# Three reorderings in the opening stage of a fused sliding-window attention and leaky-ReLU kernel

## The chip, the cores and the metric

The kernel runs on one core of a Trainium2 chip. TensorE (PE in the profile; PEld for its weight loads) multiplies matrices, VectorE (DVE), ScalarE (ACT) and GpSimd (POOL) work on elements, and SyncE (SP) only issues transfers here. Transfers that must change type on the way (float32 in memory, bfloat16 on the chip) are issued by POOL and travel in one software queue; the plain ones are issued by SP and travel in one hardware queue. Both queues are served by the same 16 DMA engines. Each engine, SP included, runs its instructions in the order in which the program names them, and waits on semaphores for the others.

The metric is the device time of one execution in microseconds. The kernel before takes 308.22 us, the median of three runs from 307.94 to 308.43.

## The reference

Eight batches of eight heads, 576 tokens, 64 dimensions a head: attention in a band of 32 tokens to either side, and then a feed-forward layer with a leaky ReLU.

```python
scores = (1.0 / np.sqrt(D)) * np.matmul(q, k.transpose(0, 1, 3, 2))
mask = np.abs(pos[:, None] - pos[None, :]) <= 32
scores = np.where(mask, scores, -1000000000.0)
scores = scores - np.max(scores, axis=-1, keepdims=True)
attn = np.exp(scores)
attn = attn / (np.sum(attn, axis=-1, keepdims=True) + 1e-09)
x = np.matmul(attn, v).transpose(0, 2, 1, 3).reshape(B * S, H * D)   # 4608 x 512
h = x @ w_in                                                        # 512 x 2048
g = np.maximum(0.01 * h, h)
return (g @ w_out).astype(np.float32)                               # 2048 x 512
```

## The kernel before, in words

All of the order is written out by hand: the program is one long list of calls, and each call appends its instructions to the engines that it uses. Heads are taken in pairs (`NPAIR` is 4), so that two heads of 64 fill 128 partitions. Batch 0 and batch 1 are each cut into two halves of 288 tokens; a step of attention is one half of one pair, and steps 0 to 15 cover the two batches. Steps 0 to 3 are the first half of batch 0, 4 to 7 its second half, 8 to 11 the first half of batch 1. The other six batches go in blocks of 64 tokens and are not touched here.

One step `i` runs through these functions:

- `load_qk(b, p)` issues two transfers on SP, queries (`qf`) and keys (`kf`) of pair `p`, 288 KB each. With the argument `behind`, the named engine first writes one element of the target tile, so that SP's transfer waits until that engine has come to this place in its own order.
- `cast_qk` makes bfloat16 copies `qb` and `kb` (line 298); for batch 1 the queries on DVE, the keys on POOL.
- `transposes` turns both on PE (lines 340 and 344) and copies them out on ACT (line 352). `place_keys` spreads the keys of batch 1 into `kbd` on DVE (line 371).
- `score(i)` multiplies them (lines 440 and 447), ACT takes the exponential (line 452), POOL or DVE multiplies by the mask (line 454).
- `sums(i)` is `row_sums` on PE (line 479) and `inverse` on DVE, a reciprocal (line 509). For step 3 the sums are made in another way: `row_sums_by_quarters` (line 490), a short reciprocal (line 495), and `spread` (line 501, in float32), which brings the inverses back to full shape. `make_rows` prepares two constant tiles for that on POOL (lines 194 to 197).
- `product(i)` multiplies by the values (line 524) and `scaled(i)` multiplies by the inverse sums and writes `xT` (line 543).

The values arrive by `load_cast_v` (line 147, POOL's queue, one transfer a head), the weights by `load_w_in` (line 727, four chunks of 512 columns) and `load_w_out` (line 731, four chunks of 512 rows), also POOL's queue.

The feed-forward layer takes the tokens in groups; group `g` of the first four is one half of a batch. `h_mms` (line 567) makes one tile of h, 128 columns of w_in by 288 tokens, from four slices `c` of 128 dimensions; slice `c` needs the pair `c` of heads. `h_first(0)` makes the first four tiles of group 0 slice by slice, as a generator: each `next` emits one more part, so that the program can put other PE work between the slices. The four tiles take the four buffers of the pool `mmps`, which the transposes and the sums of steps 1 and 2 have used before. `o_pair` (line 653) makes the first two tiles of the output, in eight parts of four matmuls; part `(j, n)` needs chunk `n` of w_out. Before each part it calls `spend`, which inserts attention work of batch 1 by a count of turns.

The pools `"x"` and `"s"` in `xps` have one buffer each: a product waits until `scaled` has read the one before, and `row_sums` waits until the reciprocal before it has read its sums (for step 4, until `scaled(3)` has read what `spread` wrote).

Around line 837, after the first group, the program casts the loads of batch 1: DVE casts queries 0 and 1 there, and queries 2 and 3 in `second_pair(0)` and `second_pair(1)`. Behind the cast of queries 3 DVE has `place_keys` for pair 2, eight clearing writes of `set_ones` and `clear_k` (lines 261 to 267), and the reciprocal of step 8.

Of the kernel before, what the change touches and what calls it, by code (L numbers as in the profile page):

```python
# [16 lines left out]
def kernel(  # L17
# [15 lines left out]
    nc = tc.nc  # L33
# [7 lines left out]
    NPAIR = H // 2  # L41
# [26 lines left out]
    def load_qk(b, p, behind=None):  # L68

        for into, src, name in ((qf, q, "qf"), (kf, k, "kf")):
            t = fload.tile([128, 2 * RUN * D], FP32, name=f"{name}{p}")
            if behind is not None:
                behind.memset(t[0:1, 0:1], 0.0)
                behind = None
            heads = src[b, 2 * p:2 * p + 2]
            if b == 0:

                into[b, p] = t[:, 0:NB * D]  # L80
                nc.sync.dma_start(
                    out=into[b, p], in_=heads.rearrange("a (p c) d -> (a p) (c d)", c=NB))
                continue
            t = t[0:96].rearrange("p (a r) -> p a r", a=2)
            if b < BY_DMA:
                nc.sync.dma_start(out=t, in_=heads.rearrange("a (p c) d -> p a (c d)", c=RUN))
            elif into is qf:
                nc.sync.dma_start(
                    out=t.rearrange("p a (g e) -> p a g e", g=3),
                    in_=heads.rearrange("a (g p c) d -> p a g (c d)", g=3, c=2),  # L90
                )
            else:
                nc.sync.dma_start(
                    out=t.rearrange("p a (c d) -> p a c d", d=D),
                    in_=heads.rearrange("a (c p) d -> p a c d", p=96),
                )
            into[b, p] = t
# [45 lines left out]
    def load_cast_v(b, p, heads=range(2)):  # L143

        for a in heads:
            r = slice(64 * a, 64 * a + 64)
            nc.gpsimd.dma_start(  # L147
                out=vbd[b % 2][r, p, :, r],
                in_=v[b, 2 * p + a].rearrange("(c p) d -> p c d", p=64),
            )  # L150
# [42 lines left out]
    def make_rows():  # L193
        nc.gpsimd.memset(to_rows, 0.0)
        for a in range(2):
            nc.gpsimd.memset(to_rows[64 * a:64 * a + 64, 96 + 16 * a:112 + 16 * a], 1.0)
        nc.gpsimd.tensor_copy(
            out=from_rows.rearrange("p (u m) -> p u m", m=64),
            in_=ident_f[:, 0:128:16].unsqueeze(2).to_broadcast([128, 8, 64]),
        )  # L200
# [175 lines left out]
    def where(i):  # L376
        return i // 8, (i // 4) % 2, i % 4
# [6 lines left out]
    def score_blocks(i):  # L384
        p, bs = i % NPAIR, blocks_of(i)
        n = 2 * 64 * len(bs)
        lo = 512 * (i % 2)
        sc = ps[:, lo:lo + n].rearrange("p (a w c i) -> p a w c i", a=2, c=2, i=32)
        for w, (b, m) in enumerate(bs):
            tok = qz[b % 2][:, p, m // 3].rearrange("p a (c i) -> p a c i", c=2)  # L390
            at = 32 * (m % 3)
            nc.tensor.matmul(  # L392
                sc[:, :, w], kz[b % 2][:, p, 64 * m:64 * m + 128],
                tok[:, :, :, at:at + 32], start=True, stop=True,
            )
        e = attn.tile([128, 2 * HALF], BF16, name="e")
        nc.scalar.activation(out=e[:, 0:n], in_=ps[:, lo:lo + n], func=AF.Exp, scale=scale)  # L397
        pr = prob[:, i % NPROB].rearrange("p n i -> p (n i)")[:, 0:n]
        nc.gpsimd.tensor_mul(pr, e[:, 0:n], band.rearrange("p w c i -> p (w c i)")[:, 0:n])  # L399
        probs[i] = pr.rearrange("p (a w i) -> p a w i", a=2, i=64)  # L400
# [28 lines left out]
    def score(i, masked_by=nc.gpsimd):  # L429
        if i >= OLD:  # L430
            return score_blocks(i)
        b, hf, p = where(i)
        tok = qT[b][:, p, hf * HALF:hf * HALF + HALF]
        if b == 0:

            for a, n_, m in ((0, 0, 0), (1, 1, 0), (0, 0, 1), (1, 1, 1), (0, 0, 2),
                             (0, 1, 0), (1, 0, 0), (0, 1, 1), (1, 0, 1), (1, 0, 2)):
                blk, i0, n = WIN[hf][n_][m]
                r = slice(64 * a, 64 * a + 64)
                nc.tensor.matmul(  # L440
                    ps_v[r, n_, i0:i0 + n], first_keys[p][r, 64 * blk:64 * blk + 64],
                    tok[r, i0:i0 + n], start=True, stop=True,
                )
        else:
            for n_, blocks in enumerate(WIN[hf]):
                for blk, i0, n in blocks:
                    nc.tensor.matmul(  # L447
                        ps_v[:, n_, i0:i0 + n], kbd[b % 2][:, p, blk],
                        tok[:, i0:i0 + n], start=True, stop=True,
                    )  # L450
        e = attn.tile([128, 2 * HALF], BF16, name="e")
        nc.scalar.activation(out=e, in_=ps[:, P0:P0 + 2 * HALF], func=AF.Exp, scale=scale)  # L452
        pr = prob[:, i % NPROB]
        masked_by.tensor_mul(  # L454
            pr.rearrange("p n i -> p (n i)"), e, mask[hf].rearrange("p n i -> p (n i)"),
        )
        probs[i] = [pr, None, None]
# [27 lines left out]
    def row_sums_by_quarters(i):  # L485
        s = xps.tile([128, 512], FP32, name="s")
        pr = probs[i][0]
        for j in range(4):
            for n in range(2):
                nc.tensor.matmul(  # L490
                    s[:, 0:QUART], to_rows[:, 96 - 32 * j:224 - 32 * j],
                    pr[:, n, QUART * j:QUART * j + QUART],
                    start=(j == 0 and n == 0), stop=(j == 3 and n == 1),
                )
        nc.vector.reciprocal(quarters, s[:, 0:QUART])
        probs[i][2] = s

    def spread(i):
        s = probs[i][2]
        for j in range(4):  # L500
            nc.tensor.matmul(
                s[:, 128 + QUART * j:128 + QUART * j + QUART], from_rows[:, 128 * j:128 * j + 128],
                quarters, start=True, stop=True,
            )
        probs[i][2] = s[:, 128:128 + HALF]
# [11 lines left out]
    def product(i):  # L517

        b, hf, p = where(i)
        pr = probs[i][0]  # L520
        x = xps.tile([128, 512], FP32, name="x")[:, 0:HALF]
        parts = [(n_, *block) for n_ in range(2) for block in WIN[hf][n_]]
        for n_, blk, i0, n in parts:
            nc.tensor.matmul(  # L524
                x[:, i0:i0 + n], vbd[b % 2][:, p, blk, :], pr[:, n_, i0:i0 + n],
                start=(blk == parts[0][1]), stop=(blk == parts[-1][1]), skip_group_check=True,
            )
        if i in (1, 2, 3):

            to = kept[i] if i < 3 else recip.tile([128, HALF], FP32, name="r")  # L530
            nc.scalar.activation(out=to, in_=x, func=AF.Copy)
            x = to
        probs[i][1] = x
# [7 lines left out]
    def scaled(i):  # L541
        _, x, r = probs.pop(i)
        nc.vector.tensor_mul(place(i), x, r)
# [20 lines left out]
    def h_mms(g, f, h, cs):  # L564
        t0, n = GROUPS[g]
        for c in cs:
            nc.tensor.matmul(  # L567
                h[:, 0:n], w_in_bf[:, c, ts(f, 128)], xT[:, c, t0:t0 + n],
                start=(c == 0), stop=(c == DMC - 1),
            )  # L570
# [42 lines left out]
    def h_first(g):  # L613

        hs = [mmps.tile([128, 512], FP32, name="mm", tag="mm") for _ in range(4)]
        yield hs[0]
        for c in range(DMC):
            for f in range(4):
                h_mms(g, f, hs[f], (c,))
            if c == DMC - 1:  # L620
                for f in range(4):
                    h_out(g, f, hs[f])
            yield
# [102 lines left out]
    def load_w_in(f0, f1):  # L726
        nc.gpsimd.dma_start(out=w_in_bf[:, :, f0:f1], in_=w_in_r[:, :, f0:f1])  # L727
# [37 lines left out]
    cast_qk(0, 3, nc.scalar, nc.gpsimd)  # L765
    load_cast_v(0, 3, (1,))
    load_w_in(512, 1024)
    load_w_in(1024, 1536)
    sums(1)
    score(2, masked_by=nc.vector)  # L770
    next(first)
# [2 lines left out]
    product(0)  # L774
    scaled(0)
    make_rows()
    score(3)
    sums(2)
    product(1)
    score(4)  # L780
    product(2)
    row_sums_by_quarters(3)
    scaled(1)
    scaled(2)
    load_w_in(1536, 2048)
    clear_on_act(kbd[1][:, 1])
    h0 = h_first(0)
    h = next(h0)
    next(h0)
    product(3)  # L790
    score(5)
    spread(3)
    scaled(3)
    next(h0)
    next(h0)
    for p in range(NPAIR):
        load_qk(1, p, nc.gpsimd if p == 0 else None)
    load_w_out(0)
    nc.gpsimd.memset(kbd[1][:, 2], 0.0)
# [39 lines left out]
    clear_vf(2)  # L839
    cast_qk(1, 1, nc.vector)  # L840
    load_cast_v(1, 0)
    load_cast_v(1, 1, (0,))
    next(band_parts)
    for p in (2, 3):
# [123 lines left out]
```

## Time and profile before

| What | Before |
|---|---|
| median of three runs | 308.22 us |
| profiled execution, its own time | 308.76 us |
| span in its trace | 307.1 us |
| PE busy | 298.0 us (97%) |
| DVE busy | 221.7 us (72%) |
| ACT busy | 204.1 us (66%) |
| POOL busy | 201.5 us (66%) |
| granted TensorE clock | 1.00 |

The profile is one execution taken by the hardware profiler. Its times count from the start of the span; a row of a timeline gives the start, the duration, the engine, the line, the operation, the tiles, the count, and in brackets the idle time of that engine just before, with what ended it. Rows that begin with an `x8` or the like are several instructions merged. The duration of a merged PE row runs to the modelled end of its last matmul, so the next row starts before it ends; what PE spends is read from start to start. A transfer appears as its issue; "DMA to landing" is the time from that issue to the arrival of the last byte.

### The profile page before, as it was taken

What the parts mean: (1) busy time and instruction counts of PE and PEld (TensorE: products, weight loads), DVE (VectorE), ACT (ScalarE), POOL (GpSimd) and SP (SyncE); (2) the same over time, 40 slices, a digit from 0 to 9 for tenths busy, and PEclk for the clock granted to TensorE, in tenths of its full rate; (3) what the DMA queues carried; (4) which work ended last, traced back from release to release, by engine and by line L of the source; (5) the groups of instructions that cost most, each with busy time, mean ns of one, the idle gap of its engine ahead of it and who ended that gap; (6) DMA issues with size and microseconds to landing.
All of it is one profiled execution on the core that took longest, in us unless ns stands there. A gap on an engine that the chain in (4) does not pass through costs nothing.

```text
span 307.1 us, 6942 instructions
## 1 busy us (share of the span) xinstructions
PE 298.0 (97%) x2616; PEld 193.5 (63%) x2646; DVE 221.7 (72%) x302; ACT 204.1 (66%) x423; POOL 201.5 (66%) x258
## 2 busy tenths in 40 slices
PE   8799999999999999999999999999999999999996
PEld 3577855676757777676768685858555555444643
DVE  6879579597888987897799777898689766743000
ACT  7876964564946677685858585849589548843731
POOL 8989799867999996889577366579757533110000
PEclk9999999999999999999999999999999999999999
DMA  7999999998999999999969984994950110001002
GB/s 248 205 183 268 264 152 218 218 209 145 208 186 215 191 256 188 190 192 228 208 151 237 226 177 113 204 204 106 196 121 1 36 68 36 0 34 72 34 31 74
DMA packets 121506, 48.31 MB, mean 157 GB/s; under 512 B 96256, under 2 KB 115968, under 8 KB 121472
## 3 DMA queue, kind: packets, MB, share of 16 engines
q1 hardware_dynamic: 107776, 42.48, 67.9%
q0 software_dynamic: 13696, 5.38, 14.5%
q8 instruction: 21, 0.34, 0.5%
q14 instruction: 13, 0.11, 0.1%
HBM read 36.70 MB, written 9.44 MB: 150 GB/s over the span
## 4 chain that ended last, share of the span: by engine, by line
PE 86%; DMA 6%; POOL 5%; issue 1%; ACT 1%; POOLq 0%; ACTq 0%
PE mm L637 38%; PE mm L567 36%; DMA w_out_bf<-in_moe_w_out_dram 6%; PE ps L392 4%; PE s L410 2%; POOL set L147 2%; PE x L410 2%; PE mm L653 2%; POOL w_in_bf L727 1%; PE x L524 1%; POOL prob L454 1%; PE ps L447 0%; POOL kb L298 0%; ACT gT L575 0%; PE s L479 0%
## 5 line engine op out<-in xcount | busy, mean ns | idle before, releaser
L567 PE MATMUL mm<-xT,w_in_bf 128*128 128x256 bf16 (+3 forms) x956 | 133.5, 294 | 0.2
L637 PE MATMUL mm<-w_out_bf,gT 128*128 128x512 bf16 (+2 forms) x537 | 122.5, 373 | 1.3
L419 DVE RECIPROCAL r<-r 128x256 f32<-128x256 f32 (+1 forms) x56 | 95.0, 1696 | 34.3 <-ACT r L418 33.7
L567 PEld LDWEIGHTS <-w_in_bf 128*128 128x128 bf16 x960 | 91.4, 98 | 29.6
L399 POOL TENSOR_TENSOR prob<-e,band 128x512 bf16<-128x512 bf16 (+1 forms) x56 | 62.6, 1118 | 56.8 <-ACT e L397 55.6
L637 PEld LDWEIGHTS <-gT 128*128 128x128 bf16 x560 | 52.1, 98 | 54.1
L575 ACT ACTIVATE gT<-mm 128x288 bf16<-128x288 f32 (+2 forms) x112 | 49.9, 479 | 12.4 <-PE mm L567 9.9
L397 ACT ACTIVATE e<-ps 128x512 bf16<-128x512 f32 (+1 forms) x56 | 32.4, 579 | 27.6 <-PE ps L392 24.6
L642 ACT ACTIVATE o_sb<-mm 128x512 f32<-128x512 f32 (+2 forms) x35 | 20.5, 585 | 39.2 <-PE mm L637 38.9
L598 ACT ACTIVATE gT<-mm 128x512 bf16<-128x512 f32 x64 | 35.7, 596 | 5.3 <-PE mm L567 3.9
L509 DVE RECIPROCAL r<-s 128x288 f32<-128x288 f32 x13 | 25.4, 1957 | 3.8 <-PE s L476 2.4
L423 DVE TENSOR_TENSOR xT<-x,r 64x256 bf16<-64x256 f32 (+1 forms) x56 | 24.4, 436 | 3.7 <-PE mm L567 0.5
L298 POOL CAST kb<-kf 96x768 bf16<-96x768 f32 (+1 forms) x30 | 25.0, 832 | 3.0 <-DMA kf<-in_k_dram 2.5
L423 DVE TENSOR_TENSOR xT<-s,r 64x256 bf16<-64x256 f32 (+1 forms) x56 | 24.4, 435 | 3.3
L324 DVE COPY set<-kT 64x576 bf16<-64x576 bf16 x48 | 21.4, 446 | 1.7 <-DMA kT<-qb 0.8
L392 PEld LDWEIGHTS <-set 128*128 128x128 bf16 x216 | 16.8, 98 | 9.2
L392 PE MATMUL ps<-set 128*128 128x128 bf16 x216 | 21.2, 219 | 0.0
L303 POOL CAST set<-vbuf 128x640 bf16<-128x640 f32 x24 | 17.2, 717 | 4.5 <-DMA vbuf<-in_v_dram 2.8
L298 POOL CAST qb<-qf 96x768 bf16<-96x768 f32 x24 | 19.7, 820 | 0.1
L454 POOL TENSOR_TENSOR prob<-e,mask 128x576 bf16<-128x576 bf16 x13 | 16.5, 1275 | 2.9 <-ACT e L452 2.8
L410 PEld LDWEIGHTS <-set 128*128 128x128 bf16 x432 | 18.0, 98 | 0.5
L304 POOL CAST set<-vbuf 64x512 bf16<-64x512 f32 x24 | 14.6, 610 | 1.5
(104 smaller groups left out, 242.2 us busy)
## 6 DMA issues: line engine op xcount, KB each, us to landing
qf<-in_q_dram SPq DMA_DIRECT2D x32, 288.0 KB, 5.5
kf<-in_k_dram SPq DMA_DIRECT2D x32, 288.0 KB, 6.1
out_dram<-o_sb SPq DMA_DIRECT2D x35, 256.0 KB, 2.9
vbuf<-in_v_dram SPq DMA_DIRECT2D x15, 256.0 KB, 4.6
w_in_bf<-in_moe_w_in_dram POOLq DMA_DIRECT2D x4, 512.0 KB, 8.4
w_out_bf<-in_moe_w_out_dram POOLq DMA_DIRECT2D x4, 512.0 KB, 15.6
vbuf<-in_v_dram SPq DMA_DIRECT2D x10, 192.0 KB, 4.4
set<-in_v_dram POOLq DMA_DIRECT2D x16, 72.0 KB, 6.4
```

The costliest lines, as they stand in the source:

```text
L298: eng.tensor_copy(out=to, in_=tok)
L392: nc.tensor.matmul(sc[:, :, w], kz[b % 2][:, p, 64 * m:64 * m + 128], tok[:, :, :, at:at + 32], start=True, stop=True,)
L397: nc.scalar.activation(out=e[:, 0:n], in_=ps[:, lo:lo + n], func=AF.Exp, scale=scale)
L399: nc.gpsimd.tensor_mul(pr, e[:, 0:n], band.rearrange("p w c i -> p (w c i)")[:, 0:n])
L410: nc.tensor.matmul(x[:, a, w], vw[b % 2][:, p, m, a:a + 2].rearrange("p n d -> p (n d)"), pr[:, a, w], start=True, stop=True,)
L419: nc.vector.reciprocal(r[:, 0:n], r[:, 0:n])
L423: nc.vector.tensor_mul(xT[rows, p, t0:t0 + n].rearrange("p (w i c) -> p w c i", i=32, c=2), x[rows, a].rearrange("p (w c i) -> p w c i", c ...
L509: nc.vector.reciprocal(r, probs[i][2])
L567: nc.tensor.matmul(h[:, 0:n], w_in_bf[:, c, ts(f, 128)], xT[:, c, t0:t0 + n], start=(c == 0), stop=(c == DMC - 1),)
L575: nc.scalar.activation(out=to, in_=h, func=AF.Prelu, alpha=0.01)
L598: nc.scalar.activation(out=gT[:, f - 1:f + 1, t0:t0 + 256], in_=hh.rearrange("p (f t) -> p f t", f=2), func=AF.Prelu, alpha=0.01,)
L637: nc.tensor.matmul(o[:, lo:hi], gT[:, f, t0:t0 + 128], w_out_bf[:, f, lo:hi], start=(f == 0), stop=(f == FFC - 1),)
```

## The change

Three things are moved; no computation is added or left out.

- In `h_first`, the first slice is cut in two: the generator now also stops ahead of the fourth tile. The calls are moved: the first three tiles of slice 0 stand ahead of `row_sums_by_quarters(3)`, the fourth behind it, slice 1 stands ahead of `spread(3)`, slice 2 directly behind `scaled(3)`. `scaled(1)` now stands ahead of the row sums of step 3 instead of behind.
- `load_w_in(1024, 1536)` is issued behind `make_rows()`.
- The queries and keys of pair 3 of batch 1 are no longer loaded with those of pairs 0 to 2, but behind POOL's two issues of `load_cast_v(1, 0)`, with POOL as the engine that SP has to wait for.

```diff
@@ h_first
         for c in range(DMC):
             for f in range(4):
+                if c == 0 and f == 3:
+                    yield
                 h_mms(g, f, hs[f], (c,))
@@
     load_w_in(512, 1024)
-    load_w_in(1024, 1536)
     sums(1)
@@
     make_rows()
+    load_w_in(1024, 1536)
     score(3)
     sums(2)
     product(1)
     score(4)
     product(2)
+    h0 = h_first(0)
+    next(h0)
+    next(h0)
+    scaled(1)
     row_sums_by_quarters(3)
-    scaled(1)
     scaled(2)
     load_w_in(1536, 2048)
     clear_on_act(kbd[1][:, 1])
-    h0 = h_first(0)
-    h = next(h0)
     next(h0)
     product(3)
     score(5)
+    next(h0)
     spread(3)
     scaled(3)
     next(h0)
-    next(h0)
-    for p in range(NPAIR):
+    for p in range(NPAIR - 1):
         load_qk(1, p, nc.gpsimd if p == 0 else None)
@@
     cast_qk(1, 1, nc.vector)
     load_cast_v(1, 0)
+    load_qk(1, NPAIR - 1, nc.gpsimd)
     load_cast_v(1, 1, (0,))
```

## The prediction

> **What bounds the kernel now.** I read the page first, then the chain that ended last, then the timelines of PE and DVE over the first 60 us, where all the edits lie, and last the landings of single transfers.
>
> ```profile
> span 307.1 us, 6942 instructions
> PE 86%; DMA 6%; POOL 5%; issue 1%; ACT 1%; POOLq 0%; ACTq 0%
> 100.00:150.00 50.00, 49.68 (x463) 36.24 (x467) 42.36 (x55) 36.30 (x75) 41.98 (x52) 1.00 1.12 207
> 24.57 17.14 DMA w_out_bf<-in_moe_w_out_dram
> 41.74 1.89 PE mm L653 x8
> ```
>
> The chain says that PE sets the end, and the row from 100 to 150 us (second column PE) that it is busy 49.68 of 50 us there. So what PE loses or gains in the opening stays to the end. One DMA stands in the chain: the third chunk of w_out, issued at 24.57, lands at 41.71, and PE starts the part that needs it at 41.74.
>
> Two places can move. The first is the work around the sums of step 3:
>
> ```profile
> 15.68 0.41 PE L524 MATMUL x<-prob,set 128*128 128x96 bf16 x5
> 16.67 0.42 PE L490 MATMUL s<-prob,set 128*128 128x72 bf16 x8 [0.58 <-POOL prob L454]
> 16.93 0.66 PE L567 MATMUL mm<-xT,w_in_bf 128*128 128x288 bf16 x4
> 18.11 1.11 PE L501 MATMUL s<-set 128*128 128x72 f32 x8
> 19.06 1.14 PE L567 MATMUL mm<-xT,w_in_bf 128*128 128x288 bf16 x8
> 20.04 0.41 PE L479 MATMUL s<-prob,ones_bd 128*128 128x288 bf16 x2
> 14.95 1.96 DVE L509 RECIPROCAL r<-mm 128x288 f32<-128x288 f32 x1 [0.44 <-PE mm L479]
> 17.13 0.61 DVE L495 RECIPROCAL set<-s 128x72 f32<-128x72 f32 x1 [0.22 <-PE s L490]
> 19.33 0.46 DVE L543 TENSOR_TENSOR xT<-r,s 128x288 bf16<-128x288 f32 x1 [0.79 <-PE s L501]
> ```
>
> PE waits 0.58 us for the mask of step 3 (POOL, line 454) and then runs without a gap. The second place is the meeting of PE and DVE at the loads of batch 1's fourth pair:
>
> ```profile
> 39.39 1.19 DVE L298 CAST qb<-qf 96x768 bf16<-96x768 f32 x1 [0.96 <-DMA qf<-in_q_dram]
> 40.51 0.90 DVE L371 COPY set<-kT 64x576 bf16<-64x576 bf16 x2
> 41.59 0.54 DVE L261 MEMSET set<- 128x576 f32 x1 [0.18 <-DMA set<-in_v_dram]
> 43.66 0.11 DVE L267 MEMSET set<- 128x64 uint32 x1
> 43.91 1.96 DVE L509 RECIPROCAL r<-s 128x288 f32<-128x288 f32 x1
> 46.84 0.46 DVE L543 TENSOR_TENSOR xT<-x,r 128x288 bf16<-128x288 f32 x1
> 47.74 1.96 DVE L509 RECIPROCAL r<-s 128x288 f32<-128x288 f32 x1 [0.44 <-PE s L479]
> 40.13 1.03 PE L653 MATMUL mm<-w_out_bf,gT 128*128 128x512 bf16 x4
> 49.76 0.42 PE L479 MATMUL s<-prob,ones_bd 128*128 128x288 bf16 x2
> ```
>
> DVE already waits 0.96 us for the fourth queries. Behind that cast it has a nearly closed list up to the reciprocal of step 9 at 47.74, which ends at 49.70; PE's sums of step 10, which need its buffer, start at 49.76. The slack of the whole list is small: 0.18 before 41.59, 0.14 before 43.91 and 0.44 before 47.74.
>
> **The change part by part.** *Three first tiles ahead of the sums.* Product 2 takes PE from 15.68 to about 15.92 (five matmuls at the pitch of 0.05 us that the row's neighbours show). Three tiles of slice 0 cost 3 x 0.1225 = 0.37 us (eight in 0.98 from 19.06 to 20.04) and fit before 16.67. The fourth would wait for the buffer that DVE's reciprocal frees at 16.91, which is why it stays behind; nothing waits for it that is not later anyway. So PE is at product 3 about 0.37 us early. It does not keep all of that. The short reciprocal now follows `scaled(1)`, (0.46, as in the row at 19.33), so it runs from about 17.35 to 17.95 and does not end at 17.74. Slice 1 (0.49) covers this, and `spread` starts at about 18.16, 0.05 later than before. From its start to that of `scaled(3)` it was 19.33 - 18.11 = 1.22, and that row lasts 0.46, so the sums of step 4, which need its buffer, can start at 18.16 + 1.22 + 0.46 + 0.02 = 19.86 instead of 20.04. Gain: 0.18 us, bounded by zero and 0.37.
>
> *Third chunk of w_in behind `make_rows`.*
>
> ```profile
> 12.56 1.53 POOL L727 DMA_DIRECT2D w_in_bf<-in_moe_w_in_dram  x2
> 15.35 2.51 POOL L454 TENSOR_TENSOR prob<-e,mask 128x576 bf16<-128x576 bf16 x2
> L727 POOL DMA_DIRECT2D w_in_bf<-in_moe_w_in_dram x2: 767/775/783, 12.6 to 13.3; - x2
> DMA to landing us min/median/max: 8.0/8.9/9.8
> 24.44 0.65 PE L567 MATMUL mm<-xT,w_in_bf 128*128 128x288 bf16 x4
> ```
>
> POOL does the same work between 13.3 and 15.35 in another order, so the mask at 15.35 does not move. The chunk is issued at about 14.6 instead of 13.3. It landed at 13.3 + 9.8 = 23.1, behind the second (12.6 + 8.0 = 20.6), and its queue keeps it behind that one; at worst it lands at 14.6 + 9.8 = 24.4. Its first reader is the ninth tile at 24.44, now 24.26. I take zero; the ends are 0 and 0.15.
>
> *The fourth pair's load.* This edit decides. In POOL's order the write that SP waits for is moved past the four issues of w_out, the clears, two casts of keys and two issues of values. SP has nothing else to issue until 44.2, so no transfer is held behind it.
>
> ```profile
> 33.82 0.82 POOL L298 CAST kb<-kf 96x768 bf16<-96x768 f32 x1 [1.65 <-DMA kf<-in_k_dram]
> 34.59 2.27 POOL L147 DMA_DIRECT2D set<-in_v_dram  x3
> L86 SPq DMA_DIRECT2D qf<-in_q_dram x1: 400/400/400, 23.3 to 23.3; - x1
> DMA to landing us min/median/max: 16.0/16.0/16.0
> L86 SPq DMA_DIRECT2D qf<-in_q_dram x1: 333/333/333, 20.4 to 20.4; - x1
> DMA to landing us min/median/max: 6.5/6.5/6.5
> L86 SPq DMA_DIRECT2D kf<-in_k_dram x1: 396/396/396, 20.8 to 20.8; - x1
> DMA to landing us min/median/max: 7.7/7.7/7.7
> L88 SPq DMA_DIRECT2D qf<-in_q_dram x1: 313/313/313, 44.2 to 44.2; - x1
> DMA to landing us min/median/max: 4.2/4.2/4.2
> 43.97 0.42 PE L344 MATMUL tp<-ident,kb 96*128 96x96 bf16 x6
> L298 DVE CAST qb<-qf x7: 453/546/1191, 4.1 to 39.4; 96x768 bf16<-96x768 f32 x4, 128x576 bf16<-128x576 f32 x3
> ```
>
> Before, the fourth queries were issued at 23.3, waited in line, and landed 16.0 later, at 39.3. Now POOL, held until 33.82 by the landing of the second keys, finishes the two value issues at 34.59 + 2 x 0.757 = 36.1, and SP issues at 36.2, when its queue is almost empty. The bounds for issue to landing: 3.1 us (it lands at 39.3 as before, still in line behind the third keys), 4.2 (the load at 44.2, with only small value pieces in the other queue), 6.5 (the load at 20.4, same bytes and same form, into an empty SP queue while POOL's queue is full of weight chunks). At 36.2 three chunks of w_out are still queued, so the last row is the nearest and I take it: landing 42.7.
>
> The cast then ends at 42.7 + 0.55 = 43.25 (median of the casts). The list behind it, from 40.51 to the end of the 0.46 at 46.84, is 6.79 us, or 6.47 without the two waits. So the reciprocal of step 9 can start at 43.27 + 6.5 = 49.8 instead of 47.74: 2.05 us late, and PE's sums of step 10 with it. The same rows follow each other at once for steps 10 and 11, so nothing is made up. The keys of the pair, issued at 36.7, land by their own row 7.7 later at 44.4; POOL's cast (0.82) ends at 45.2 and PE's transposes of them come at 45.3 instead of 43.97. That is 1.3 late and lies inside the 2.05.
>
> What the move buys: w_out's third chunk no longer shares with the fourth pair. PE would be ready for it at 40.13 + 1.03 - 0.18 = 40.98 instead of 41.74. But PE then meets the late reciprocal, and its 0.77 us become waiting there. The terms on PE's path: -0.18 and up to -0.59 up to 41 us, and then a wait of up to 2.8 us that ends 2.05 us later than the old time. Sum: +2.05.
>
> **The profiled execution** took 308.76 us, its span 307.1 and 1.66 around it; 308.76 + 2.05 = 310.8. The median of the runs, 308.22, is 0.54 lower, so I predict 310.3 there.
>
> A rule against this reading. The row is the 6.5 us of the load at 20.4. The Trainium skill, DMA: Bandwidth & Descriptors, "Queues, rings and completion order" and "Latency and other measured facts", says that each DMA engine takes the queues that have work in turn, packet by packet, and gives about 0.6 us to the first byte on the hardware queue. By that the fourth queries, issued at 36.2, would be in line before the third keys have finished and land at about 39.3 after all. That makes it the second rival below. The 6.5 us speak against it, though the first load had shared its way with nothing of its own queue.
>
> **The rivals.**
> 1. *Landing in time (faster).* One mechanism: the fourth queries still land at 39.3, right behind the third keys, while w_out's third chunk comes early enough for PE at 40.98. DVE's list then closes up: the sums come 0.77 earlier, the waits of 0.14 and 0.44 go, and 0.18 of PE's early transposes is added; the reciprocal of step 9 starts up to 0.72 early. 308.22 - 0.7 = 307.5. It needs the landing before about 39.5. For it: third keys and fourth queries were in one line before. Against: the 6.5 us.
> 2. *Little changes (same).* The landing lies near 40.4, which the 4.2 us row gives. The cast ends at 41.0 and the reciprocal of step 9 starts at 47.5, or the w_out chunk is no earlier because one DMA engine is late for both queues; then PE starts it at 41.74 still and DVE's slack hides the rest. 308.0, from 307.8 to 308.6. The point from which it turns slower by 0.2% (0.6 us, about what a measurement of this kernel can tell from no change) is a landing of 41.2: 41.2 + 0.57 + 6.5 = 48.3.
> 3. *The third chunk of w_in comes late.* At most 0.15 us at the ninth tile, and DVE's list hides it. Alone it gives 308.2.
>
> **How the numbers follow.** Forecast 0.60; little changes 0.22; in time 0.15; the rest, 0.03, is worse than the forecast. Range of the forecast itself: 309.0 (landing 41.2) to 311.0, the top being 2.05 plus 0.64 for a cast that again takes 1.19 instead of 0.55, on 308.22. Eight times in ten: down to 307.7, which leaves out a part of the first rival, and up to 311.0. Faster 0.16, same 0.21, slower 0.63.
>
> **What would show it.** In the profile after: three tiles of line 567 ahead of line 490 and the gap of 0.58 gone; sums of step 4 at 19.9; the memset of line 75 on POOL at 36.1, and 6 us or more from SP's issue to landing; the cast of line 298 on DVE at about 42.7 with an idle time of some 4 us behind the DMA; PE waiting at the transposes of pair 3 and at the sums of step 10 for the reciprocal, starting near 51.8 instead of 49.76. A landing before 41 makes the prediction wrong; so would a part of DVE's list that can shrink.

## The result, and the profile after

The kernel with the three edits takes 310.50 us (median of six runs, 310.10 to 312.27); the kernel before, on the same chip, 308.13 (six runs, 307.94 to 309.07). The ratio is 1.0076, with a 95% interval from 1.0053 to 1.0099: 1.6 to 3.1 us slower. The profiled execution took 310.16 us with a span of 308.5.

The page of the kernel after (the `span` line, and the chain that ended last by engine), and two lines of its waits (total, times, longest):

```profile
span 308.5 us, 6942 instructions
PE 83%; POOL 9%; issue 3%; ACT 2%; DMA 2%; DVE 1%; POOLq 0%; ACTq 0%; DVEq 0%
POOL kb L298 <- DMA kf<-in_k_dram: 4.1, 3, 3.1
DVE qb L298 <- DMA qf<-in_q_dram: 3.8, 2, 3.2
```

w_out's load has left the chain, and POOL has taken its place. The longest single waits of the casts at line 298 are now 3.2 us on DVE and 3.1 us on POOL. The fourth pair's issue and landing, from the views of its tiles:

```profile
L86 SPq DMA_DIRECT2D qf<-in_q_dram x1: 313/313/313, 35.2 to 35.2; - x1
DMA to landing us min/median/max: 6.1/6.1/6.1
L86 SPq DMA_DIRECT2D kf<-in_k_dram x1: 443/443/443, 35.6 to 35.6; - x1
DMA to landing us min/median/max: 8.4/8.4/8.4
```

The timeline of DVE and then PE of the kernel after at the places that the prediction quoted of before:

```profile
16.62 1.35 DVE L543 TENSOR_TENSOR xT<-set,r 128x288 bf16<-128x288 f32 x1
17.89 0.59 DVE L495 RECIPROCAL set<-s 128x72 f32<-128x72 f32 x1
41.84 0.56 DVE L298 CAST qb<-qf 96x768 bf16<-96x768 f32 x1 [3.15 <-DMA qf<-in_q_dram]
42.31 0.90 DVE L371 COPY set<-kT 64x576 bf16<-64x576 bf16 x2
48.74 1.95 DVE L509 RECIPROCAL r<-s 128x288 f32<-128x288 f32 x1
15.96 0.54 PE L567 MATMUL mm<-xT,w_in_bf 128*128 128x288 bf16 x3
16.47 0.42 PE L490 MATMUL s<-prob,set 128*128 128x72 bf16 x8
18.02 0.65 PE L567 MATMUL mm<-xT,w_in_bf 128*128 128x288 bf16 x4 [0.34 <-DVE xT L543]
20.27 0.42 PE L479 MATMUL s<-prob,ones_bd 128*128 128x288 bf16 x2
40.38 2.75 PE L655 MATMUL mm<-w_out_bf,gT 128*128 128x512 bf16 x12
44.92 0.43 PE L344 MATMUL tp<-ident,kb 96*128 96x96 bf16 x6 [1.29 <-POOL kb L298]
50.74 0.42 PE L479 MATMUL s<-prob,ones_bd 128*128 128x288 bf16 x2
```

The three tiles stand ahead of the sums of step 3 and fill the old gap of 0.58 us. But `scaled(1)` on DVE lasts 1.35 us there, PE waits 0.34 for it at 18.02, and the sums of step 4 come at 20.27 instead of 20.04. At 40.38 twelve matmuls of the output run through without the old wait for w_out. Then PE stands 1.29 us at the transposes of the fourth keys, and the sums of step 10 start at 50.74 instead of 49.76, right behind DVE's reciprocal (48.74 + 1.95).

Where the 1.40 us between the two profiled executions come from, cut at three instructions of PE that both have:

| Stretch | before | after | difference |
|---|---|---|---|
| start to the sums of step 2 | 14.49 | 14.29 | -0.20 |
| sums of step 2 to sums of step 4 | 5.55 | 5.98 | +0.43 |
| sums of step 4 to sums of step 10 | 29.72 | 30.47 | +0.75 |
| sums of step 10 to the end | 257.34 | 257.76 | +0.42 |

The first line is start-up: in the kernels below the sums of step 2 come anywhere from 14.27 to 15.75 us, though little or nothing differs ahead of them. A good part of this is the granted clock of TensorE. In the four profiles where they come latest (15.61 to 15.75: only the keys late, queries cast on ACT, two chunks of w_out left out, load moved less far) it is 0.50 from 10 to 14 us; in nine others, the two of this table among them, it is 1.00 there, and they come at 14.27 to 14.95. The rows of before and of the kernel with only the keys late (stretch, length, busy time of PE, PEld, DVE, ACT and POOL, clock, DMA share, GB/s):

```profile
10.00:14.00 4.00, 3.06 (x73) 1.94 (x74) 3.27 (x4) 3.68 (x7) 4.00 (x6) 1.00 1.76 181
10.00:14.00 4.00, 3.94 (x84) 2.51 (x81) 3.25 (x3) 2.73 (x5) 3.53 (x6) 0.50 1.92 179
```

Why the clock falls there in some executions and not in others is open. The 29.72 of before holds its wait of 0.59 for w_out. The third line is therefore a net of two things, and the experiments separate them. The medians of the two kernels lie 2.37 us apart, so about 1 us of the measured difference stands in neither of these two traces.

### The profile page after: what moved, and what is told of

The parts are those of the page before. It is cut to its first block, busy times and chain, and to the rows that moved or that the text cites. A ratio compares the mean times of both kernels' runs of the same rounds, so it can differ in the third digit from the quotient of the medians.

```text
span 308.5 us, 6942 instructions
## 1 busy us (share of the span) xinstructions
PE 298.0 (97%) x2616; PEld 193.0 (63%) x2646; DVE 223.9 (73%) x302; ACT 203.9 (66%) x423; POOL 201.8 (65%) x259
## 4 chain that ended last, share of the span: by engine, by line
PE 83%; POOL 9%; issue 3%; ACT 2%; DMA 2%; DVE 1%; POOLq 0%; ACTq 0%; DVEq 0%
PE mm L639 36%; PE mm L567 35%; PE ps L392 4%; POOL set L147 3%; PE s L410 2%; PE x L410 2%; DMA set<-kb 2%; POOL kb L298 1%; PE mm L655 1%; POOL prob L454 1%; POOL set L828 1%; POOL w_out_bf L733 1%; PE x L524 1%; DVE xT L543 1%; PE ps L447 0%
```

## The experiments

Theory A is the prediction's: the late load of the fourth pair carries the loss, through DVE's list behind the cast of its queries. Theory B puts it on the new order around the sums of step 3. All diffs are against the kernel before. All ratios are to the kernel before on the same chip. Two further kernels leave out work, ran once each, and serve for their traces alone.

| Kernel | Ratio | 95% interval |
|---|---|---|
| the change | 1.0076 | 1.0053 to 1.0099 |
| only the load | 1.0057 | 1.0036 to 1.0077 |
| only the order | 0.9996 | 0.9979 to 1.0013 |
| only the w_in chunk | 0.9996 | 0.9968 to 1.0024 |
| only the keys late | 1.0003 | 0.9976 to 1.0030 |
| only the queries late | 1.0070 | 1.0048 to 1.0092 |
| queries cast later on DVE | 1.0133 | 1.0099 to 1.0166 |
| queries cast on ACT | 1.0035 | 1.0016 to 1.0054 |
| load moved less far | 1.0031 | 1.0004 to 1.0058 |
| three tiles alone | 0.9992 | 0.9974 to 1.0010 |
| three tiles, keys late | 0.9996 | 0.9977 to 1.0015 |

**Each part alone.** The load:

```diff
-    for p in range(NPAIR):
+    for p in range(NPAIR - 1):
         load_qk(1, p, nc.gpsimd if p == 0 else None)
...
     load_cast_v(1, 0)
+    load_qk(1, NPAIR - 1, nc.gpsimd)
     load_cast_v(1, 1, (0,))
```

> Only the fourth pair's load is moved; the order around the sums of step 3 and the w_in chunk are as before. Theory A (the late load carries the loss): SP issues the queries near 35 to 36 us, they land some 6 us later, DVE's cast waits 2 to 4 us, the reciprocal of step 9 starts 1 to 2 us later than 47.74, and the time is 309.2 to 310.3 us. Theory B (the new order around the sums of step 3 carries it, because scaled(1) on DVE takes 1.35 us there instead of 0.46): this kernel stays within 0.5 us of before.

The ratio of 1.0057 is 1.8 us (1.1 to 2.4). The timeline of DVE and PE:

```profile
42.55 0.56 DVE L298 CAST qb<-qf 96x768 bf16<-96x768 f32 x1 [3.75 <-DMA qf<-in_q_dram]
49.45 1.95 DVE L509 RECIPROCAL r<-s 128x288 f32<-128x288 f32 x1
44.27 0.43 PE L344 MATMUL tp<-ident,kb 96*128 96x96 bf16 x6 [0.52 <-POOL kb L298]
48.16 0.42 PE L479 MATMUL s<-prob,ones_bd 128*128 128x288 bf16 x2 [0.40 <-DVE r L509]
51.45 0.42 PE L479 MATMUL s<-prob,ones_bd 128*128 128x288 bf16 x2 [0.61 <-DVE r L509]
```

The cast waits 3.75 us, the reciprocal of step 9 starts at 49.45 instead of 47.74, and PE waits for DVE's reciprocals twice, as theory A has it. The order alone:

```diff
+                if c == 0 and f == 3:
+                    yield
...
     product(2)
+    h0 = h_first(0)
+    next(h0)
+    next(h0)
+    scaled(1)
     row_sums_by_quarters(3)
-    scaled(1)
...
-    h0 = h_first(0)
-    h = next(h0)
     next(h0)
     product(3)
     score(5)
+    next(h0)
     spread(3)
     scaled(3)
     next(h0)
-    next(h0)
```

> Only the order around the sums of step 3 is changed. Theory A: scaled(1) is slow again (1.2 us or more), the sums of step 4 start about 0.4 us later, but PE then waits that much less for w_out's third chunk at 41.7 us, so the time is within 0.3 us of before. Theory B: the 0.4 us stay, 0.4 to 2 us slower.

From the sums of step 2 to those of step 4 this kernel takes 5.98 us, just as the whole change does, so the 0.43 us are real. Its total does not differ from before: the interval reaches to 0.4 us slower, which leaves of theory B's range only the lower edge. PE meets no wait for w_out afterwards (28.99 us from the sums of step 4 to those of step 10), as expected. The w_in chunk alone:

```diff
-    load_w_in(1024, 1536)
...
     make_rows()
+    load_w_in(1024, 1536)
```

> Only the third chunk of w_in is issued behind make_rows. Both theories: it lands behind the second chunk as before, near 22 to 24 us, ahead of its first reader at 24.4; no difference beyond 0.3 us.

No difference. But its profiled execution also shows no wait for w_out (28.97 us between the same two sums), with the fourth pair loaded as before. The 0.59 us of the profiled execution before is thus not there in every kernel that loads the pair at its old place; what the load's move could have bought was smaller than that profile shows.

**Which half of the pair.** The load is issued with its keys alone, or its queries alone, at the late place (a new argument of `load_qk` names which of the two it issues; the diff is that of the late keys):

```diff
-    for p in range(NPAIR):
-        load_qk(1, p, nc.gpsimd if p == 0 else None)
+    for p in range(NPAIR):
+        load_qk(1, p, nc.gpsimd if p == 0 else None, (0, 1) if p < NPAIR - 1 else (0,))
...
     load_cast_v(1, 0)
+    load_qk(1, NPAIR - 1, nc.gpsimd, (1,))
```

> Of the fourth pair only the keys are loaded late (at the place of the change); its queries stay in line with the other pairs. Nothing else is changed. Theory A (DVE's list behind the cast of the queries and POOL's cast of the keys both hold PE, about equally): the queries land near 39.3, DVE's list is not held, the keys land 6 us after their issue near 41.5, which POOL needs only at about 42.1, so the time is between 0.4 us faster and 0.2 us slower than before. Rival C (any late load of the pair holds PE at its transposes): 0.5 to 1 us slower.

> Counterpart of the run with only the keys late: the keys of the fourth pair stay in line with the other pairs, its queries alone are loaded at the place of the change. Theory A (DVE's list behind the cast of the queries carries the loss): the queries land near 41 to 42 us, the cast waits, the reciprocal of step 9 starts 0.5 to 1.5 us late, 0.5 to 1.5 us slower than before. Rival (it takes both, or POOL's cast of the keys): within 0.3 us of before.

Late keys alone show no cost (1.0003; the interval reaches 0.9 us, but PE does not wait at the transposes in the trace), late queries alone cost as much as the whole change (1.0070). In the kernel with late queries DVE's cast and PE's waits read:

```profile
43.06 1.58 DVE L298 CAST qb<-qf 96x768 bf16<-96x768 f32 x1 [4.07 <-POOL kb L298]
44.70 0.43 PE L344 MATMUL tp<-ident,qb 96*128 96x96 bf16 x6 [1.01 <-DVE qb L298]
49.70 0.42 PE L479 MATMUL s<-prob,ones_bd 128*128 128x288 bf16 x2 [1.24 <-POOL vbuf L119]
52.99 0.42 PE L479 MATMUL s<-prob,ones_bd 128*128 128x288 bf16 x2 [0.60 <-DVE r L509]
```

The cast takes 1.58 us instead of 0.56. The queries land at 42.6 (issue 36.59, 6.0 to landing), while POOL makes its cast of the keys and the mask of step 9, and the cast ends behind both. The profile puts PE's wait of 1.24 us down to POOL's vbuf, which has no part in these sums; they need the buffer of DVE's reciprocal of step 8, which ran from 47.74 to 49.63. POOL:

```profile
42.14 0.84 POOL L298 CAST kb<-kf 96x768 bf16<-96x768 f32 x1
42.92 1.29 POOL L454 TENSOR_TENSOR prob<-e,mask 128x576 bf16<-128x576 bf16 x1
```

So a late cast is not only late. It also falls under POOL's work, and the 2.2 us of this kernel are not the price of the landing alone.

**Is it DVE's list?** If the list behind the cast carries the loss, the cast has to leave its place in it while the load stays late. Both kernels here have the late load of the change besides the diff. First, to a later place on DVE:

```diff
-        if p + 2 < NPAIR:
-            cast_qk(1, p + 2, nc.vector, nc.gpsimd if p == 0 else None)
+        if p == 0:
+            cast_qk(1, p + 2, nc.vector, nc.gpsimd)
...
             clear_k(0, nc.vector)
+            cast_qk(1, 3, nc.vector, None)
```

> The load of the fourth pair is late as in the change (nothing else of it), and DVE's cast of its queries is moved behind place_keys for pair 2 and the clearing writes, just ahead of the reciprocal of step 8. Theory A: the landing is as late as before this move (some 6 us), but DVE's list no longer waits for it; PE is held only at the transposes, by the keys, for about 0.5 us; the time is -0.2 to +0.6 us against before. Rival (the lateness of the data itself holds PE): as slow as the late load alone, +1.2 us or more.

This missed both expectations: 1.0133, the slowest kernel here, 4.1 us. The timeline of DVE and PE, and POOL's beside it:

```profile
44.35 2.20 DVE L298 CAST qb<-qf 96x768 bf16<-96x768 f32 x1
46.61 0.43 PE L344 MATMUL tp<-ident,qb 96*128 96x96 bf16 x6 [3.29 <-DVE qb L298]
47.32 3.37 PE L653 MATMUL mm<-w_out_bf,gT 128*128 128x512 bf16 x8
44.09 0.82 POOL L298 CAST kb<-kf 96x768 bf16<-96x768 f32 x1 [2.96 <-DMA kf<-in_k_dram]
44.87 1.26 POOL L454 TENSOR_TENSOR prob<-e,mask 128x576 bf16<-128x576 bf16 x1
```

DVE's list was free of the wait, but the cast came at 44.35, in the middle of POOL's cast and mask, and lasted 2.20 us; PE stood 3.29 us. That is not the whole loss. Behind this stand the granted clock of TensorE fell, and the eight matmuls at 47.32 took 3.37 us, where before they take 1.89:

```profile
48.00:49.00 1.00, 1.00 (x3) 0.30 (x2) 0.99 (x3) 0.27 (x1) 1.00 (x2) 0.50 0.89 118
```

Of its six runs the one with a mean clock of 1.00 took 310.46 us, 1.8 above the kernel before; the other five, at 0.982 to 0.995, took 312.5 to 314.2. So this kernel says nothing on the list, and its 4.1 us are not the price of the cast alone. Second, to ACT:

```diff
-        if p + 2 < NPAIR:
-            cast_qk(1, p + 2, nc.vector, nc.gpsimd if p == 0 else None)
+        if p == 0:
+            cast_qk(1, p + 2, nc.vector, nc.gpsimd)
...
             clear_half(0, 0, 0, nc.scalar)
+            cast_qk(1, 3, nc.scalar, None)
```

> The load of the fourth pair is late as in the change (nothing else of it); the cast of its queries is taken from DVE's list and given to ACT, behind its clearing of half a query tile, where ACT is free from about 42 us on. Theory A (the loss is DVE's list standing behind the cast): the queries land 6 us after their issue as before, DVE goes straight from place_keys to the clearing writes, its reciprocal of step 9 is on time, PE waits only about 0.5 us for the keys, and the time is within 0.5 us of before. Rival (the late data hold PE whichever engine casts): 1.2 us slower or more, as with the late load alone.

1.0035, that is 1.1 us (0.5 to 1.7) where the late load alone costs 1.8 (1.1 to 2.4). The intervals overlap, so the totals do not show that the move to ACT gave anything back, and the time is not shown to be within the 0.5 us expected. The trace shows more: DVE no longer holds anything, and its reciprocal of step 9 now waits for PE. What is left is the keys, with a wait of 1.19 us where about 0.5 was expected:

```profile
49.67 1.96 DVE L509 RECIPROCAL r<-s 128x288 f32<-128x288 f32 x1 [0.65 <-PE s L479]
45.01 0.82 POOL L298 CAST kb<-kf 96x768 bf16<-96x768 f32 x1 [3.06 <-DMA kf<-in_k_dram]
45.89 0.43 PE L344 MATMUL tp<-ident,kb 96*128 96x96 bf16 x6 [1.19 <-POOL kb L298]
```

Issued behind the queries the keys land 8.4 us after their issue here (7.1 to 8.4 in the four kernels that issue both late beside full weight chunks); issued alone, in the kernel with only the keys late, 6.0. So there are two holds, DVE's list and POOL's cast of the keys, and they overlap. In the profile of the change both end at the same time: the reciprocal frees the buffer at 50.69, and PE, counted from the transposes at 44.92 with the work of before (49.76 - 43.97 = 5.79), comes to 50.71. In the kernel with only the load late the keys land after 7.1 us, and there DVE's list ends last: PE waits for its reciprocals. Neither "only DVE" nor "any late data" holds. Theory A is right about the first hold; which of the two is worth more by itself is not settled.

**Why 6 us.** With the late load, and with two of w_out's chunks not loaded, so that POOL's queue is nearly empty when the late load is issued:

```diff
     load_w_out(1)
-    load_w_out(2)
...
-            load_w_out(3)
...
+    nc.vector.memset(w_out_bf[:, 8:16, :], 0.0)
```

> The fourth pair's load is late as in the change, and the third and fourth chunks of w_out are not loaded: DVE clears them instead, so the output lacks their part. Theory A (the 6 us from issue to landing are the time to get past the weight chunks queued by POOL): with that queue nearly empty the queries land 3 to 4.5 us after their issue. Rival (a transfer into an idle queue takes 6 us in any case): 5.5 us or more.

```profile
L86 SPq DMA_DIRECT2D qf<-in_q_dram x1: 313/313/313, 37.0 to 37.0; - x1
DMA to landing us min/median/max: 4.0/4.0/4.0
```

4.0 us, in one execution, against 6.0 to 6.3 in the five kernels (the change among them) that load the fourth queries late beside full weight chunks. The trace's records of single pieces show that it is the time to the first one: in the change no data piece starts in SP's queue between 34.86 and 38.72 us, with the issue at 35.24, so 3.5 us pass; here the first piece comes at 38.13, 1.1 after the issue at 36.99. It is 3.5 to 3.6 us in all seven kernels that issue a part of the fourth pair late beside full chunks, and about 1.0 for the load at 44.24 of the kernel before, when the chunks are through.

It is not the empty queue that costs this. In the kernel with only the load late, pieces of the third pair arrive in SP's queue until 36.91, 1.0 us behind the issue at 35.92, and the first new piece still comes 3.5 us after the issue; with the queries cast on ACT or later on DVE it is the same. The second test moves the load less far, while the pairs ahead of it are still under way:

```diff
             load_w_out(3)
+            load_qk(1, NPAIR - 1, nc.gpsimd)
```

> The load of the fourth pair is moved behind POOL's issue of the fourth chunk of w_out only, some 4 us later than before and 8 to 9 us earlier than in the change, while the pairs ahead of it are still under way in SP's queue. Theory A (the loss comes from the queue running empty and starting again behind the weights): it lands near 39 to 40 us as before, within 0.3 us of before. Rival (any later issue costs): 0.5 us slower or more.

1.0031, that is 1.0 us (0.1 to 1.8): the middle fits the rival, but the interval does not exclude theory A, and the kernel is not shown to cost less than the late load alone. The queries, issued at 28.6, landed 12.6 us later at 41.2 in an execution that began 1.2 us late (sums of step 2 at 15.66), and PE waited 0.67 us for w_out in it. Before, they landed at 39.3. What the less far move pays for is not settled by this.

**Why `scaled(1)` is slow.** Theory D: POOL's mask of step 4 stands in its way. The order of the change, and step 4 left unmasked:

```diff
+        pr = prob[:, i % NPROB]
+        if i == 4:
+            nc.scalar.activation(
+                out=pr.rearrange("p n i -> p (n i)"), in_=ps[:, P0:P0 + 2 * HALF], func=AF.Exp, scale=scale)
+            probs[i] = [pr, None, None]
+            return
```

> The order around the sums of step 3 as in the change, nothing else of it; the mask of step 4 is left out (ACT writes its exponentials straight to where the masked ones go), so that POOL is free from about 16.5 us on. Theory D (scaled(1) on DVE, which reads two tiles in SBUF, is held by POOL's mask of step 4): scaled(1) takes 0.4 to 0.6 us instead of 1.35 and slice 1 on PE starts without a wait. Rival E (it is held by its own inputs or by the place in the list): still 1.2 us or more.

DVE, and then PE's sums, of this kernel (its line 548 is line 543, 484 is 479):

```profile
17.16 0.39 DVE L548 TENSOR_TENSOR xT<-set,r 128x288 bf16<-128x288 f32 x1
14.83 0.42 PE L484 MATMUL mm<-prob,ones_bd 128*128 128x288 bf16 x2
20.23 0.41 PE L484 MATMUL s<-prob,ones_bd 128*128 128x288 bf16 x2
```

0.39 us instead of 1.35, and 5.40 from sums to sums. In the change the instruction ran from 16.62 to 17.97, and POOL's masks of steps 3 and 4 until 17.65; so it ended 0.32 us behind them. The two long casts above ended just as closely behind POOL's mask, by 0.43 (44.64 after 44.21) and 0.42 us (46.55 after 46.13): it looks like waiting for POOL to end, and then running at about the usual speed. POOL in the change:

```profile
15.14 2.51 POOL L454 TENSOR_TENSOR prob<-e,mask 128x576 bf16<-128x576 bf16 x2
```

The Trainium skill, SBUF — State Buffer, "Who interferes with whom", says that a DVE instruction with two inputs in SBUF contends with a GpSimd instruction that reads SBUF, and that whichever starts first holds the shared port for its whole length. `scaled(1)` reads two SBUF tiles and POOL's mask reads two. The 1.35 and 0.39 us agree with it.

**A better order.** The three tiles alone, with `scaled(1)` where it was, and the same with only the keys late:

```diff
+                if c == 0 and f == 3:
+                    yield
...
     product(2)
+    h0 = h_first(0)
+    next(h0)
+    next(h0)
     row_sums_by_quarters(3)
     scaled(1)
...
-    h0 = h_first(0)
-    h = next(h0)
     next(h0)
```

> Only the three first tiles stand ahead of the sums of step 3; scaled(1), spread and the slices 1 and 2 keep their places. Theory D (the change's new order lost 0.43 us between the sums of step 2 and those of step 4 by DVE's scaled(1) standing under POOL's mask): from sums to sums 5.2 to 5.4 us instead of 5.55 before and 5.98 in the change; the time 0 to 0.4 us below before. Rival E (putting tiles ahead does not pay in itself): 5.5 us or more.

> A version meant to beat both: the three first tiles ahead with the rest of that order as before, and of the fourth pair only the keys late. Theory: no wait of PE for w_out's third chunk, none for the fourth pair, and 5.2 to 5.4 us from the sums of step 2 to those of step 4; 0.2 to 0.7 us faster than before. If the gains do not add up it equals before.

From the sums of step 2 to those of step 4 the two take 5.41 and 5.24 us instead of 5.55. In the first, PE waited 0.22 us for w_in's first chunk ahead of the three tiles:

```profile
16.76 0.54 PE L567 MATMUL mm<-xT,w_in_bf 128*128 128x288 bf16 x3 [0.22 <-DMA w_in_bf<-in_moe_w_in_dram]
```

The gain of 0.14 to 0.31 us is there in the trace, and the totals (0.9992 and 0.9996, each with an interval of some 0.2% to both sides) cannot tell it from nothing; the second missed its expectation of 0.2 to 0.7 us. Neither version is shown to beat the kernel before.

## Why the prediction was right, point by point

The direction, the cause and the time (310.3 forecast, 310.5 measured) came out. That the time was met to 0.2 us is luck. The terms of the opening came to less than half of the forecast (0.98 of 2.05 us); of the rest of the measured 2.37, 0.42 lies behind the opening, where the prediction had nothing, and about 1 us stands in no trace.

- **Three tiles ahead: wrong in sign.** The step that failed is the one that let `scaled(1)` last 0.46 us, "as in the row at 19.33". That row reads one of its inputs from PSUM and keeps its 0.46 though a mask of POOL runs beside it; `scaled(1)` reads both from SBUF. At its new place it took 1.35, and the forecast gain of 0.18 became a loss of 0.43. With POOL out of the way the same order gives 5.40 instead of 5.55, a gain of 0.15. The arithmetic of the step held; the cover on DVE did not.
- **The third chunk of w_in: right.** It lands at 14.4 + 7.9 = 22.3, and alone it makes no difference.
- **Issue and landing of the fourth queries: right in kind, large by 1.4 us.** Issue 35.2 instead of 36.2, since POOL got the second keys 0.9 earlier (its cast at 32.89 instead of 33.82); 6.1 us to landing instead of 6.5. The row of the load at 20.4 was the right neighbour. The landing at 41.3 is hardly behind the 41.2 that the prediction named as its turning point, and by its own sum (41.3 + 0.57 + 6.5 = 48.4) would make the reciprocal of step 9 0.6 us late. But the cast started only at 41.84, 0.5 behind the landing, which the prediction had not allowed for and no run explains; 42.7 was forecast.
- **DVE's list: right.** From the start of `place_keys` to the reciprocal of step 9 it took 48.74 - 42.31 = 6.43 us; 6.5 was forecast. The reciprocal came 1.00 late, not 2.05, mainly because the cast started 0.9 earlier than forecast.
- **The keys: too small.** They were priced as lying inside DVE's delay. In the profile of the change they set PE's time as much as DVE did, and with the cast given to ACT, where they are the only hold left, the kernel is still 1.1 us slower.
- **What the move buys: over-priced.** PE did reach w_out's third chunk without a wait, but so did a kernel in which the load had not moved.
- **The sum.** For the profiled execution 310.8 was forecast and 310.16 measured. The terms up to the sums of step 10 come to +0.98 and not +2.05. Behind that the prediction had nothing, and the trace has +0.42. Part of this, 0.3 us, is a wait of PE at about 130 us for keys that a DMA transposes; the chain of the kernel after shows that transfer (5.17 is its length, not the wait):

```profile
124.84 5.17 DMA set<-kb
```

In the kernel with only the load late that last stretch is 0.61 us longer than before, with only the keys late 1.3 (258.7), with only the queries late it is equal (257.31). Why it moves from one profile to the next is open. So is why the six runs of the change spread over 2.2 us, of which the profiled execution lies near the lower end.

The rule weighed in the prediction, from the Trainium skill's DMA: Bandwidth & Descriptors ("Latency and other measured facts": about 0.6 us to the first byte on the hardware queue), does not hold in this stage: the records show 3.5 us beside full weight chunks and 1.1 without two of them. The first rival fell with it: the prediction calls the rule its second rival, but a landing at 39.3 is the first.

## What to carry to other kernels

A transfer that is held back does not take its old place in line again. Beside a queue full of weight chunks it took 3.5 us to its first piece here, whether or not its own queue still had work, so price it from a load of the same trace that started under the same neighbours, and then ask what stands behind its first reader on that engine. A duration taken from another row is only good if the neighbours are the same: here a product of DVE that reads two SBUF tiles, and a long cast, took three to four times as long under POOL's work. And look at the granted clock before a loss is put down to the edit.

## What the runs showed of the hardware that was not expected

The same cast of queries on DVE (96 x 768 from float32) took 0.56 us with POOL idle, 1.58 when POOL's cast and mask were under way, and 2.20 when it began inside POOL's cast and the mask followed at once. (The 1.19 of the kernel before, beside POOL's issues of values, was not tested.) The product in `scaled(1)` went from 0.39 to 1.35 under POOL's mask, while the reciprocals of DVE, which read one tile, from PSUM, kept their 1.96 us beside the same masks. The granted clock of TensorE was 0.50 for a few microseconds in some executions: for some 3.4 us right behind PE's wait of 3.29 us in the kernel with the queries cast later, and around 10 to 14 us in four profiles of the opening. There the sums of step 2 came up to 1.5 us later than in the earliest profile, more than most of the edits here are worth.
